# ALiBi and mask tables by 64x64 quadrant matmuls in the first two batches of a fused attention and MLP kernel

## The chip, the cores and the metric

The kernel runs on one core of one Trainium2 chip, and the metric is device time in microseconds (us). A core has a matrix engine (PE, with its weight loads shown apart as PEld), a vector engine (DVE), a scalar engine (ACT), a general engine (POOL), a queue engine (SP) that here only issues transfers, and 16 DMA engines. PE reads operands from the on-chip memory SBUF and writes sums to PSUM, which DVE and ACT read. Each engine works through its own instructions in the order in which they were written; engines wait for one another by semaphores.

## The reference

```python
scores = scale * np.matmul(q, k.transpose(0, 1, 3, 2))        # 8 batches, 8 heads, 576 x 576
rel = pos[:, None] - pos[None, :]
slopes = 2.0 ** (-8.0 * (np.arange(H) + 1) / H)
bias = slopes[:, None, None] * (-np.abs(rel))                 # ALiBi
mask = (rel >= 0) & (rel < 128)                               # causal, sliding window
attn = softmax(np.where(mask, scores + bias, -1e9))
x = (attn @ v)        # to 4608 tokens x 512
h = x @ w_in                                                  # 512 x 2048
out = (h * np.clip(h + 3, 0, 6) / 6) @ w_out                  # 2048 x 512, float32
```

Each query sees itself and the 127 keys before it. So a tile of 128 keys is seen by two tiles of queries: its own ("diagonal", lower triangle) and the next one ("off", the other triangle).

## The kernel before, in words

**Order.** The whole program is written out by hand (`manual_schedule` over all engines): the order of the calls is the order on every engine. `first_batch()` does the attention of batch 0, `second_batch()` that of batch 1 with the first MLP matmuls between, and `segment()` the other six batches, one pair of heads (`g`) at a time, with MLP steps put between by `fill(n)`. An "up" step (`moe_up`, line 532) is four matmuls of 128x512, an ACT relu (line 556) and a DVE product (line 557); a "down" step (`moe_down`, line 587) is four matmuls more. All MLP work of the kernel goes through `fill`.

**Attention of a pair of heads in batches 0 and 1.** Two PSUM tiles of 128 x 2 x 512 (`score`) are used in turn by `score_banks()`. One takes the four diagonal blocks of both heads (`scores_diag`, line 346: eight matmuls, 64 contraction rows, 128 keys, 128 queries), the other the off blocks and the last 64 keys (`scores_off`, lines 372 and 378: ten matmuls). ALiBi and mask come in two ways:

- as a table: `tab` holds slope x (key position - query base), with -2^30 where the mask is; a matmul of the identity with it (lines 321, 357, 360) puts it under the scores in PSUM. So the off blocks of batches 0 and 1 and the diagonal blocks of batch 0;
- as a bias: the diagonal blocks of batch 1 take a per-key bias in the exponential (`exp_diag`, line 425, one of 512 columns per head), and POOL then sets the masked triangle to zero (`affine_select`, line 427). The batches after 1 do this for both kinds of block.

The tables are made at the start by POOL (`base`) and DVE (line 144, eight operations of 128x256), the biases by DVE (lines 166 to 172, seventeen operations of one column). The exponentials go to memory that has no other use yet: `w_out_sb` for batch 0, `gbuf[1]` for batch 1. `attend(g)` then multiplies them with V, DVE divides by the row sum, and `back(g)` turns the result into `xT` for the MLP.

**Batches 2 to 7** already use another score layout in `scores()` (line 399): 64 contraction rows x 64 keys x 192 queries, so that four matmuls have four different quadrants of the PE array. Their rows show what quadrant matmuls do here.

**Around the change.** The first 512 columns of `w_in` come as one transfer issued by SP (`load_raw`) and are cast by POOL and ACT (`cast_raw`, line 187). Loads of `w_out` (`load_w_out`, line 190, four parts of 512 KB) are issued by POOL in `second_batch`, behind whatever POOL has to do before; part p is first read by down step p of the first token block.

Of the kernel before, what the change touches and what calls it, by code (L numbers as in the profile page):

```python
# [13 lines left out]
ALU = mybir.AluOpType  # L14
# [4 lines left out]
def kernel(  # L19
# [39 lines left out]
    tab = perm.tile([128, H, 2, 128], BF16)  # L59
# [63 lines left out]

    def constants():
# [4 lines left out]
        nc.gpsimd.iota(rel_i, pattern=[[0, 1]], base=0, channel_multiplier=1)  # L129
        base = rpool.tile([128, NT], FP32, tag="r6", name="base")  # L130
        base_i = base[:, 0:256].bitcast(INT32).rearrange("p (s c) -> p s c", s=2)
        base_b = base[:, 256:384].bitcast(BF16).rearrange("p (s c) -> p s c", s=2)
        nc.gpsimd.iota(base_i, pattern=[[128, 2], [0, 128]], base=-192, channel_multiplier=1)
        nc.gpsimd.tensor_copy(out=base_b, in_=base_i)
        biases()
        nc.gpsimd.affine_select(out=base_b[:, 1, :], in_=base_b[:, 1, :], pattern=[[1, 128]],
                                channel_multiplier=-1, base=0,
                                compare_op=ALU.is_ge, fill=-(2.0 ** 30))
        nc.gpsimd.affine_select(out=base_b[:, 0, :], in_=base_b[:, 0, :], pattern=[[-1, 128]],
                                channel_multiplier=1, base=-1,  # L140
                                compare_op=ALU.is_ge, fill=-(2.0 ** 30))
        nc.vector.memset(kTb[0][:, :, 4, LAST:128], 0.0)
        for h in range(H):
            nc.vector.tensor_scalar(out=tab[:, h, :, :], in0=base_b, scalar1=slopes[h] / scale,
                                    scalar2=0.0, op0=ALU.mult, op1=ALU.add)
# [5 lines left out]
    def memsets_later():  # L151
        for i in range(2):
            nc.gpsimd.memset(p4buf[i], 1.0)
        nc.gpsimd.memset(kTb[1][:, :, 4, LAST:128], 0.0)
# [10 lines left out]
    def biases():  # L165
        nc.vector.tensor_copy(out=rel_f, in_=rel_i)
        for h in range(H):
            nc.vector.tensor_scalar(out=bias_o[:, h:h + 1], in0=rel_f, scalar1=-192.0,
                                    scalar2=slopes[h], op0=ALU.add, op1=ALU.mult)

        for h in range(H):
            nc.vector.tensor_scalar(out=bias_d[:, h:h + 1], in0=rel_f, scalar1=-64.0,
                                    scalar2=slopes[h], op0=ALU.add, op1=ALU.mult)
# [139 lines left out]
    def diag_tabled(g):  # L313
        return g < NP

    def tables_diag(g):
        scd = score_banks()
        st[g, "scd"] = scd
        for e in range(2 if diag_tabled(g) else 0):
            t = tab[:, 2 * (g % NP) + e, 1:2, :]  # L320
            nc.tensor.matmul(scd[:, e, :].rearrange("p (j c) -> p j c", j=4), lhsT=ident,
                             rhs=t.to_broadcast([128, 4, 128]), start=True, stop=False)

    def rooms(g):
        b, hp = divmod(g, NP)
        if full(g):
            room = w_out_sb if b == 0 else gbuf[1]
            for i, nm in enumerate(("pd", "po")):
                st[g, nm] = room[:, ds(4 * hp + 2 * i, 2), :].rearrange(
                    "p e (j c) -> p e j c", j=4)  # L330
        else:
            st[g, "pd"] = ppool.tile([128, 2, 4, 128], BF16, tag="pd", name="pd")
            st[g, "po"] = ppool.tile([128, 2, 4, 128], BF16, tag="po", name="po")

    def scores_diag(g):
        rooms(g)
        b, hp = divmod(g, NP)
        qT, kT = qTb[b % 2][:, hp, :, :], kTb[b % 2][:, hp, :, :]
        first = not diag_tabled(g)
        if (g, "scd") not in st:  # L340
            tables_diag(g)
        scd = st[g, "scd"]
        for j in range(4):
            for e in range(2):
                r = slice(e * D, (e + 1) * D)
                nc.tensor.matmul(scd[:, e, ts(j, 128)], lhsT=kT[r, j, :],  # L346
                                 rhs=qT[r, j, :], start=first, stop=first or j == 3)

    def tables_off(g):
        hp = g % NP  # L350
        sco = score_banks()
        st[g, "sco"] = sco
        if full(g):
            for e in range(2):
                h = 2 * hp + e
                t = tab[:, h, 0:1, :]
                nc.tensor.matmul(sco[:, e, 128:512].rearrange("p (j c) -> p j c", j=3),  # L357
                                 lhsT=ident, rhs=t.to_broadcast([128, 3, 128]),
                                 start=True, stop=False)
                nc.tensor.matmul(sco[:, e, 0:128].rearrange("p (s c) -> p s c", s=2),  # L360
                                 lhsT=ident, rhs=tab[:, h, :, 0:64], start=False, stop=False)

    def scores_off(g):
        b, hp = divmod(g, NP)
        qT, kT = qTb[b % 2][:, hp, :, :], kTb[b % 2][:, hp, :, :]
# [521 lines left out]
```

## Time and profile before

| | |
|---|---|
| median of three runs | 320.45 us (319.79, 320.45, 320.58) |
| span of the profiled execution | 317.9 us |
| what the runs' median has around that span | 2.55 us |
| PE busy | 307.0 us, 97% |
| ACT, DVE, POOL busy | 196.8, 176.1, 138.9 us |
| granted PE clock | 1.000 |
| first batch, second batch, rest | about 0 to 24.3, 24.3 to 49.7, 49.7 to 317.9 us |

The profiled execution is shown by its span; no time beside the span is given for it. A timeline row gives start and length of a group of instructions, line, operation, output <- inputs, and in brackets how long the engine sat idle before and what ended that. The length of a PE row goes to the modelled end of its last matmul, so the rate is read from one start to the next.

### The profile page before, as it was taken

To read this page: it belongs to the slowest core of one execution; us is meant where nothing else is said; L and a number is where in the kernel's file an instruction comes from. 1 tells how busy PE (TensorE), PEld (TensorE's weight loads), DVE (VectorE), ACT (ScalarE), POOL (GpSimd) and SP (SyncE) were. 2 spreads that over 40 slices of the span, in tenths; PEclk is the share of its full clock that TensorE was granted. 3 is DMA by queue.
4 is the path that set the end of the run, shared out by engine and by line. 5 is a ranking of instruction groups with operands and counts; after the bars stand their busy time and mean duration, and the time that the engine had idled before them with its cause. 6 is when DMAs were issued, how large, how long until landed. Compare 5 with 4: busy or idle time off the path is not lost.

```text
span 317.9 us, 6980 instructions
## 1 busy us (share of the span) xinstructions
PE 307.0 (97%) x2671; PEld 163.4 (51%) x2710; DVE 176.1 (55%) x344; ACT 196.8 (62%) x338; POOL 138.9 (44%) x247
## 2 busy tenths in 40 slices
PE   8889999999999999999999999999999999999996
PEld 3565474455554445555676644454444444444443
DVE  6677676554456654566465546564656455455510
ACT  3869986877767666766667756675764244244401
POOL 7358192674594684548463854472231000000000
PEclk9999999999999999999999999999999999999999
DMA  7999999999999999999999999934112100000112
GB/s 271 264 373 215 255 236 200 236 235 198 216 265 180 222 215 212 213 196 253 186 178 219 190 206 198 228 95 57 49 29 75 66 34 33 35 33 33 66 57 77
DMA packets 131425, 52.43 MB, mean 165 GB/s; under 512 B 118976, under 2 KB 122816, under 8 KB 131392
## 3 DMA queue, kind: packets, MB, share of 16 engines
q1 hardware_dynamic: 125648, 46.15, 69.0%
q0 software_dynamic: 3696, 3.67, 7.1%
q10 hardware_dynamic: 2048, 2.16, 2.2%
q8 instruction: 21, 0.34, 0.5%
q14 instruction: 12, 0.10, 0.1%
HBM read 36.70 MB, written 9.44 MB: 145 GB/s over the span
## 4 chain that ended last, share of the span: by engine, by line
PE 90%; ACT 3%; DVE 3%; issue 2%; POOL 0%; DVEq 0%; POOLq 0%; ACTq 0%
PE hps L532 38%; PE ops L587 37%; PE score L399 3%; PE av L463 2%; PE av L455 2%; DVE avs L485 1%; PE ops L568 1%; PE w L163 1%; ACT w_out_sb L422 1%; PE score L346 1%; PE tp L269 1%; ACT r L556 1%; DVE gbuf L557 1%; PE score L301 1%; PE score L357 1%
## 5 line engine op out<-in xcount | busy, mean ns | idle before, releaser
L556 ACT ACTIVATE r<-hps,bias 128x512 f32<-128x512 f32 x144 | 98.9, 689 | 84.2 <-PE hps L532 83.9
L557 DVE SCALAR_TENSOR_TENSOR gbuf<-r,hps 128x512 bf16<-128x512 f32 x144 | 98.8, 688 | 91.6 <-ACT r L556 90.1
L532 PE MATMUL hps<-xT,w_in_sb 128*128 128x512 bf16 (+1 forms) x623 | 142.0, 358 | 1.7 <-ACT xT L519 0.3
L587 PE MATMUL ops<-w_out_sb,gbuf 128*128 128x512 bf16 x538 | 133.8, 379 | 2.3 <-issue 1.8
L532 PEld LDWEIGHTS <-w_in_sb 128*128 128x128 bf16 x640 | 59.2, 98 | 54.0 <-issue 1.5
L587 PEld LDWEIGHTS <-gbuf 128*128 128x128 bf16 x560 | 52.4, 98 | 57.5
L427 POOL TENSOR_SCALAR_AFFINE_SELECT pd<-pd 128x512 bf16<-128x512 bf16 x48 | 29.4, 631 | 35.2 <-ACT pd L425 35.2
L436 POOL TENSOR_SCALAR_AFFINE_SELECT po<-po 128x512 bf16<-128x512 bf16 x48 | 30.1, 633 | 30.8 <-ACT po L434 30.1
L596 DVE COPY osb<-ops 128x512 f32<-128x512 f32 x33 | 22.7, 688 | 23.8 <-PE ops L587 23.7
L425 ACT ACTIVATE pd<-score,bias_d 128x512 bf16<-128x512 f32 x48 | 31.1, 683 | 6.4 <-PE score L399 6.4
L434 ACT ACTIVATE po<-score,bias_o 128x512 bf16<-128x512 f32 x48 | 33.1, 690 | 0.0
L213 POOL CAST tbuf<-ldbuf 128x512 bf16<-128x512 f32 (+1 forms) x45 | 25.7, 611 | 15.7 <-issue 14.6
L474 DVE TENSOR_TENSOR avs<-av,rc 128x384 bf16<-128x384 f32 (+1 forms) x48 | 23.6, 491 | 1.6
L463 PEld LDWEIGHTS <-pd 128*128 128x128 bf16 x192 | 14.3, 97 | 8.2 <-issue 0.2
L455 PE MATMUL av<-vbuf,po 128*128 128x65 bf16 x192 | 18.0, 193 | 0.0
L206 POOL CAST vbuf<-ldbuf 128x1024 bf16<-128x1024 f32 x14 | 14.3, 1041 | 7.6 <-DMA ldbuf<-in_v_dram 7.6
L463 PE MATMUL av<-vbuf,pd 128*128 128x65 bf16 x192 | 17.3, 194 | 0.0
L455 PEld LDWEIGHTS <-po 128*128 128x128 bf16 x192 | 14.3, 98 | 3.0 <-DVE avs L474 0.5
L439 ACT ACTIVATE p4buf<-score,bias_d 128x64 bf16<-128x64 f32 x48 | 15.6, 324 | 0.0
L399 PEld LDWEIGHTS <-kTb 64*64 64x64 bf16 x480 | 9.4, 106 | 9.1 <-issue 8.5
L399 PE MATMUL score<-qTb,kTb 64*64 64x192 bf16 (+1 forms) x480 | 13.1, 234 | 0.0
L246 POOL CAST pr<-ldbuf 128x576 bf16<-128x576 f32 x18 | 11.5, 668 | 2.6 <-PE tp L238 1.3
(107 smaller groups left out, 201.7 us busy)
## 6 DMA issues: line engine op xcount, KB each, us to landing
out_dram<-osb SPq DMA_DIRECT2D x33, 256.0 KB, 3.5
ldbuf<-in_v_dram SPq DMA_DIRECT2D x31, 256.0 KB, 4.6
ldbuf<-in_q_dram SPq DMA_DIRECT2D x20, 256.0 KB, 5.0
ldbuf<-in_k_dram SPq DMA_DIRECT2D x16, 256.0 KB, 5.3
ldbuf<-in_q_dram SPq DMA_DIRECT2D x12, 288.0 KB, 6.6
ldbuf<-in_k_dram SPq DMA_DIRECT2D x12, 288.0 KB, 6.7
w_out_sb<-in_moe_w_out_dram POOLq DMA_DIRECT2D x4, 512.0 KB, 9.1
w_in_sb<-in_moe_w_in_dram POOLq DMA_DIRECT2D x3, 512.0 KB, 8.8
```

The lines of the kernel that those rows point to most:

```text
L213: nc.gpsimd.tensor_copy(out=tbuf[:m, :, j, :], in_=s[:m, j, :, :].rearrange("p (i e) d -> p i (e d)", e=2))
L399: nc.tensor.matmul(wide[e][c, ds(at, n)], lhsT=kT[r, j, c], rhs=qT[r, ds(q0, n)], start=True, stop=True)
L425: nc.scalar.activation(out=pd[:, e, :, :], in_=block_scores(g, e, False), func=ACT.Exp, bias=bias_d[:, h:h + 1], scale=scale)
L427: nc.gpsimd.affine_select(out=pd[:, e, :, :], in_=pd[:, e, :, :], pattern=[[0, 4], [1, 128]], channel_multiplier=-1, base=0, compare_op=AL ...
L434: nc.scalar.activation(out=po[:, e, :, :], in_=sc, func=ACT.Exp, bias=bias_o[:, h:h + 1], scale=scale)
L436: nc.gpsimd.affine_select(out=po[:, e, :, :], in_=po[:, e, :, :], pattern=[[0, 4], [-1, 128]], channel_multiplier=1, base=-1, compare_op=A ...
L455: nc.tensor.matmul(out_av, lhsT=po[:, e, (qt if full(g) else qt - 1) % 4, :], rhs=vb[:, qt - 1, h, :], start=True, stop=False)
L463: nc.tensor.matmul(out_av, lhsT=d, rhs=vb[:, qt, h, :], start=(qt == 0), stop=True)
L532: nc.tensor.matmul(hps[:, lo:hi], lhsT=w_in_sb[:, ks, ts(ms, 128)], rhs=xT[:, ks, ds(src, hi - lo)], start=(ks == 0), stop=(ks == n_ks - 1))
L556: nc.scalar.activation(out=r6, in_=hps, func=ACT.Relu, bias=bias3[:, 0:1], scale=1.0 / 6.0)
L557: nc.vector.scalar_tensor_tensor(out=gts[nt][:, ms, :], in0=r6, scalar=1.0, in1=hps, op0=ALU.min, op1=ALU.mult)
L587: nc.tensor.matmul(ops[nt, sub], lhsT=gts[nt][:, ms, ts(sub, 128)], rhs=w_out_sb[:, ms, :], start=(ms == 0), stop=(ms == n_ms - 1))
```

## The change

- `tab` becomes 128 x 4 x 3 x 256: for each pair, head e on partitions 64e to 64e+63, three shifts of a strip of 256 (diagonal and off triangle). POOL makes the strip from a cast of six columns with two `affine_select`s of 128x384; DVE scales it by one per-partition slope, four operations of 128x768, one before the first tables, the other three inside `first_batch`.
- Diagonal and off blocks no longer have a PSUM tile each. Half t=0 of a pair holds key tiles 0 and 1 with their diagonal and off blocks side by side, half t=1 key tiles 2, 3 and 4. `tables(g, t)` writes the table by matmuls of 64 contraction rows and 64 output partitions, one quadrant each: four of 512 columns for t=0; for t=1 twelve, in the order quadrant by quadrant, 256, 192 and 64 columns in each. `scores_full` then adds eight (t=0) or ten (t=1) quadrant matmuls of up to 192 columns.
- `exp_full(g, t)`: one exponential of 1024 columns per half, in both batches. Batch 1 loses its eight exponentials of 512 columns with bias and its eight POOL masks, and gains tables under what were its diagonal blocks.
- `biases()` moves from DVE at the start to POOL in `second_batch`, after the cast of V and ahead of `load_w_out(0)`. The zeroing of `kTb[0]` moves from DVE to POOL's `memsets_later`.
- `weights()` finds the block of the exponentials in the new layout; the matmuls with V stay the same in number and size.

```diff
     def constants():
...
-        biases()
...
+        for hp in range(NP):
+            for e in range(2):
+                nc.vector.memset(slope2[ds(e * 64, 64), hp:hp + 1], slopes[2 * hp + e] / scale)
+        nc.vector.tensor_copy(out=first, in_=first_i)
+        wide = first.rearrange("p i s -> p i s ()").to_broadcast([128, 3, 2, 128])
+        nc.gpsimd.affine_select(out=base[:, :, 0, :], in_=wide[:, :, 0, :],
+                                pattern=[[-64, 3], [1, 128]], channel_multiplier=-1, base=64,
                                 compare_op=ALU.is_ge, fill=-(2.0 ** 30))
...
-        nc.vector.memset(kTb[0][:, :, 4, LAST:128], 0.0)
-        for h in range(H):
-            nc.vector.tensor_scalar(out=tab[:, h, :, :], in0=base_b, scalar1=slopes[h] / scale,
-                                    scalar2=0.0, op0=ALU.mult, op1=ALU.add)
+        slope_table(0)
+
+    def slope_table(hp):
+        nc.vector.tensor_scalar(out=tab[:, hp, :, :],
+                                in0=base.rearrange("p i s c -> p i (s c)"),
+                                scalar1=slope2[:, hp:hp + 1],
+                                scalar2=0.0, op0=ALU.mult, op1=ALU.add)
...
+    def tables(g, t):
+        hp = g % NP
+        sc = st[g, "sc", t] = score_banks()
+        for c in range(2):
+            o = slice(c * 64, (c + 1) * 64)
             for e in range(2):
                 r = slice(e * D, (e + 1) * D)
+                src = tab[r, hp, c + 1 - e, :]
+                row = sc[o, e, :]
+                if t == 0:
+                    nc.tensor.matmul(row.rearrange("p (j c) -> p j c", j=2), lhsT=ident[r, r],
+                                     rhs=src.rearrange("p (j c) -> p j c", j=1).to_broadcast(
+                                         [64, 2, 256]), start=True, stop=False)
+                    continue
+                for at, n in ((0, 256), (256, 192), (448, 64)):
+                    nc.tensor.matmul(row[:, ds(at, n)], lhsT=ident[r, r], rhs=src[:, 0:n],
+                                     start=(at == 0), stop=False)
+
+    def scores_full(g, t):
...
+        for j in (2 * t, 2 * t + 1):
+            for c in range(2):
+                q0 = j * 128 + c * 64
+                n = min(192, S - q0)
+                for e in range(2):
+                    r = slice(e * D, (e + 1) * D)
+                    nc.tensor.matmul(sc[ds(c * 64, 64), e, ds(j % 2 * 256 + c * 64, n)],
+                                     lhsT=kT[r, j, ds(c * 64, 64)], rhs=qT[r, ds(q0, n)],
+                                     start=False, stop=(j % 2 == 1 and (t == 0 or c == 1)))
+        if t == 1:
+            for e in range(2):
+                r = slice(e * D, (e + 1) * D)
+                nc.tensor.matmul(sc[0:64, e, 448:512], lhsT=kT[r, 4, 0:64],
+                                 rhs=qT[r, 512:S], start=False, stop=True)
+
+    def exp_full(g, t):
+        at = 1024 * (1 - t)
+        nc.scalar.activation(out=room(g)[:, ds(at, 1024)], in_=st[g, "sc", t].rearrange(
+            "p e c -> p (e c)"), func=ACT.Exp, scale=scale)
...
     def first_batch():
         prepare(0, (V, A))
+        slope_table(1)
...
         prepare(1, (P, V))
+        slope_table(2)
+        slope_table(3)
         transposes(1, (V, V))
...
     def second_batch():
-        scores_diag(NP + 0)
-        exp_diag(NP + 0, 0)
-        exp_diag(NP + 0, 1)
+        scores_full(NP + 0, 0)
+        exp_full(NP + 0, 0)
...
         cast_tokens(1, "v")
-        scores_diag(NP + 2)
-        exp_diag(NP + 2, 0)
-        exp_diag(NP + 2, 1)
+        biases(nc.gpsimd)
+        scores_full(NP + 2, 0)
+        exp_full(NP + 2, 0)
...
         load_w_out(0)
         load_w_out(1)
         g = 2 * NP - 1
-        scores(g)
-        exp_diag(g, 0)
-        exp_diag(g, 1)
-        exp_off_full(g)
+        for t in range(2):
+            scores_full(g, t)
+            exp_full(g, t)
```

More of the change, by code (lines that the diff above doesn't have):

```diff
@@ L153, in memsets_later @@
             nc.gpsimd.memset(p4buf[i], 1.0)
-        nc.gpsimd.memset(kTb[1][:, :, 4, LAST:128], 0.0)
+            nc.gpsimd.memset(kTb[i][:, :, 4, LAST:128], 0.0)
         nc.gpsimd.memset(vbuf[1][:, :, :, D:W], 1.0)
@@ L163, in warm_up, with biases @@
             nc.tensor.matmul(w, lhsT=ident, rhs=rhs, start=True, stop=True)
[L165 to L173, printed above, removed]
+    def biases(eng):
+        eng.tensor_copy(out=rel_f, in_=rel_i)
+        for dst, far in ((bias_o, -192.0), (bias_d, -64.0)):
+            for h in range(H):
+                eng.tensor_scalar(out=dst[:, h:h + 1], in0=rel_f, scalar1=far,
+                                  scalar2=slopes[h], op0=ALU.add, op1=ALU.mult)
     def load_w_in(g):
@@ L311, in full @@
         return g < NB_FULL * NP
[L313 to L324, printed above, removed]
-        b, hp = divmod(g, NP)
[L326 to L343, printed above, removed]
+    def room(g):
+        b, hp = divmod(g, NP)
+        return (w_out_sb if b == 0 else gbuf[1])[:, ds(4 * hp, 4), :].rearrange(
+            "p m c -> p (m c)")
+    def tables(g, t):
[3 more added lines that the diff above has]
+            o = slice(c * 64, (c + 1) * 64)
@@ L344, in scores_diag @@
             for e in range(2):
                 r = slice(e * D, (e + 1) * D)
[L346 to L361, printed above, removed]
```

132 lines of the change are left out of this document (55 added, 77 removed).

## The prediction

> **What bounds the kernel now.** I read the page first, then the busy time by stretches, then the timelines of the first 62 us, where the change lies.
>
> ```profile
> span 317.9 us, 6980 instructions
> PE 307.0 (97%) x2671; PEld 163.4 (51%) x2710; DVE 176.1 (55%) x344; ACT 196.8 (62%) x338; POOL 138.9 (44%) x247
> PE 90%; ACT 3%; DVE 3%; issue 2%; POOL 0%; DVEq 0%; POOLq 0%; ACTq 0%
> ```
>
> ```profile
> 24.00:30.00 6.00, 5.72 (x72) 3.38 (x72) 4.53 (x7) 5.87 (x11) 4.74 (x8) 1.00 1.26 220
> 30.00:40.00 10.00, 9.89 (x80) 4.70 (x79) 6.85 (x10) 9.28 (x15) 3.33 (x5) 1.00 1.16 248
> ```
>
> PE is 97% busy and 90% of the chain that ended last. In the second batch (the two rows: length, then busy time of PE) it is idle for 0.28 of 6 and 0.11 of 10 us. From 24.3 us on, whatever PE does more comes out at the end, and time taken from ACT or POOL is worth only what PE waited for them. The sum is made on the span; the median of the runs, 320.45, has 2.55 us around it, which I keep.
>
> The first batch has a wait of its own:
>
> ```profile
> 18.87 1.14 ACT L187 CAST w_in_sb<-gbuf 128x512 bf16<-128x512 f32 x2 [1.41 <-DMA gbuf<-in_moe_w_in_dram]
> 18.90 0.61 POOL L187 CAST w_in_sb<-gbuf 128x512 bf16<-128x512 f32 x1 [4.66 <-DMA gbuf<-in_moe_w_in_dram]
> 20.60 0.59 PE L532 MATMUL hps<-xT,w_in_sb 128*128 128x512 bf16 x2
> 22.86 0.66 PE L301 MATMUL score<-ident,pr 128*128 128x128 bf16 x9 [0.18 <-ACT pr L256]
> ```
>
> ACT and POOL stand idle until the raw w_in lands at 18.87. Then come two ACT casts, the copies of xT, the cast of q and, at 22.86, the PE work that waits for it. This is why I take the first batch at nothing in both directions: what it gains before 18.87 ends at that transfer, which SP issues untouched; a loss has the 1.41 us of ACT and 0.18 us of PE idle ahead of it.
>
> **The change part by part.** *Start and first batch.*
>
> ```profile
> 2.86 1.76 DVE L144 TENSOR_SCALAR tab<-base 128x256 bf16<-128x256 bf16 x8
> 8.41 0.76 DVE L239 COPY qTb<-tp 128x576 bf16<-128x576 bf16 x1 [0.93 <-PE tp L238]
> ```
>
> Eight table operations of 256 columns took 1.76 us, 0.86 ns a column; a new one of 768 is at most 0.66 us. One replaces eight ahead of the first tables. Two stand ahead of the copy at 8.41, where DVE is idle 0.93 us: 1.32 us would make it 0.4 us late, and the chain copy, scores, exponential with it; the 1.41 us above take that up. The removed DVE biases, the two longer POOL selects and the added POOL memset lie in the same cover. Without it they would cost those 0.4 us. POOL's new wait for the six-column cast holds back only its memsets and the cast of q after them.
>
> *Batch 1 on PE, per pair.* Old blocks:
>
> ```profile
> 34.37 0.40 PE L346 MATMUL score<-qTb,kTb 64*128 64x128 bf16 x8
> 34.70 1.04 PE L532 MATMUL hps<-xT,w_in_sb 128*128 128x512 bf16 x4
> 35.57 0.33 PE L357 MATMUL score<-tab,ident 128*128 128x384 bf16 x1
> ...
> 35.95 0.22 PE L360 MATMUL score<-tab,ident 128*128 128x128 bf16 x1
> 36.11 0.20 PE L372 MATMUL score<-qTb,kTb 64*128 64x64 bf16 x2
> ...
> 36.44 1.90 PE L532 MATMUL hps<-xT,w_in_sb 128*128 128x512 bf16 x8
> ```
>
> Four MLP matmuls go from 34.70 to 35.57, 0.217 us for 512 columns. From 35.95 a table of 128 columns needs 0.054, yet the scores start at 36.11: 0.10 us are lost where the shape changes from 128 to 64 rows, and about as much on the way back. Old cost: diagonal 0.33 + 0.10 = 0.43, off 36.44 - 35.57 = 0.87 us.
>
> What quadrants do, from the scores of batch 2 (the last three rows are what overlaps 49.88 to 49.93, 49.93 to 49.95 and 49.99 to 50.00):
>
> ```profile
> 49.66 0.55 PE L399 MATMUL score<-qTb,kTb 64*64 64x192 bf16 x20
> 50.14 1.04 PE L587 MATMUL ops<-w_out_sb,gbuf 128*128 128x512 bf16 x4
> L399 PE MATMUL score<-qTb,kTb x12: 242/243/268, 49.7 to 49.9; 64*64 64x192 bf16 x12
> L399 PE MATMUL score<-qTb,kTb x15: 216/243/268, 49.7 to 49.9; 64*64 64x192 bf16 x13, 64*64 64x128 bf16 x2
> L399 PE MATMUL score<-qTb,kTb x14: 189/242/243, 49.8 to 50.0; 64*64 64x192 bf16 x10, 64*64 64x128 bf16 x2, 64*64 64x64 bf16 x2
> ```
>
> Twenty matmuls with 3,328 columns take 0.48 us to the next shape, 0.38 without the gap: 1.41 us in a row at the rate above, so four quadrants do work side by side. With three rounds of four begun by 49.93, a round of 192 columns takes 0.08 to 0.09 us.
>
> Half t=0: gap 0.10, four tables side by side 0.22, two rounds 0.17, start 0.02, gap 0.10: 0.60, that is +0.17.
>
> Half t=1 depends on whether the second and third table of a quadrant hold up the next quadrant. The last row: two matmuls of 64 columns had begun by 50.00. They follow, in the code, two of 192 (key half 0) and two of 128 (half 1) that began after 49.93 and so run to about 50.01 and 49.99. As 64-column matmuls of half 0 they would find their quadrant occupied; I read them as those of half 1, which passed two waiting ones. One waiting matmul per quadrant thus doesn't stop the others; the trace doesn't show two. Bounds: all four quadrants free, 245 + 190 ns and the gaps, 0.64 us (-0.23); strictly in order, each quadrant holds the next for 256 + 192 columns, 0.82 of tables, 1.18 us (+0.31). I take the nearest to what is shown: the third weight load of a quadrant waits for its second matmul, so the next quadrant starts 0.13 us behind; the last begins at 0.40, ends tables at 0.64 and scores, partly alongside, at 0.78: 0.98 us (+0.11).
>
> The Trainium skill's page TensorE: Matmul & The Clock Gate, section The mechanism, states that matmuls start and end in program order, "strict FIFO, no reordering". By that rule t=1 would cost the +0.31; the last row above speaks against it.
>
> *ACT and POOL in batch 1.*
>
> ```profile
> 25.36 1.27 ACT L425 ACTIVATE gbuf<-score,bias_d 128x512 bf16<-128x512 f32 x2
> 26.50 1.04 ACT L409 ACTIVATE gbuf<-score 128x1024 bf16<-128x1024 f32 x1
> 26.68 0.66 PE L301 MATMUL score<-ident,pr 128*128 128x128 bf16 x9 [0.23 <-ACT gbuf L425]
> ```
>
> Two exponentials of 512 take 1.27 us, one of 1024 takes 1.04. The 0.23 saved is on the path only here, where PE waited 0.23; so the first pair's +0.28 falls into that wait and comes to 0. Pairs two and three cost 0.28 each. The fourth has its halves back to back, all in 64x64, and saves two shape changes: 0.28 - 0.20 = +0.08. PE sum: +0.64 us. The eight masks gone from POOL are worth nothing in themselves: no PE row waits for one.
>
> *Biases ahead of the w_out loads on POOL.*
>
> ```profile
> L213 POOL CAST tbuf<-ldbuf 128x512 bf16<-128x512 f32 (+1 forms) x45 | 25.7, 611 | 15.7 <-issue 14.6
> L206 POOL CAST vbuf<-ldbuf 128x1024 bf16<-128x1024 f32 x14 | 14.3, 1041 | 7.6 <-DMA ldbuf<-in_v_dram 7.6
> 1.33 0.13 POOL L129 IOTA rel_i<- 128x1 int32 x1
> 1.41 0.34 POOL L133 IOTA base<- 128x256 int32 x1
> 40.06 1.21 POOL L427 TENSOR_SCALAR_AFFINE_SELECT gbuf<-gbuf 128x512 bf16<-128x512 bf16 x2
> 41.23 1.51 POOL L190 DMA_DIRECT2D w_out_sb<-in_moe_w_out_dram x2
> ```
>
> No row has such an operation on POOL. Casts of 512 and 1024 columns (611, 1041 ns) leave 0.18 us for one column; rows of POOL overlap by about 0.05 (41.23 - 40.06 is 1.17 for a row of 1.21), so 0.13 from start to start. Ends: 0.08 (the one-column iota, 1.33 to 1.41) and 0.18 without overlap. Seventeen: 1.4, 2.3, 3.1 us. They replace 1.17 us of masks, so w_out part 0 is issued 0.2, 1.1 or 1.9 us later; I take 1.1. Behind them parts 2 and 3 and the casts come about when they did, since 1.2 us of masks go there too. SP's loads of V for batch 2, which wait for POOL's memset after that, stay with it.
>
> ```profile
> DMA to landing us min/median/max: 11.6/11.6/11.6
> q0 software_dynamic: 1465, 1.46, 116.0%
> q0 software_dynamic: 296, 0.30, 88.1%
> 58.15 1.03 PE L587 MATMUL ops<-w_out_sb,gbuf 128*128 128x512 bf16 x4
> ```
>
> Part 3, issued at 45.89, landed 11.6 us later, at 57.5; its first reader runs at 58.15. These loads are limited by transfer: 1.46 MB from 44 to 52 us, 0.18 MB a us, and 0.15 from 53 to 55 when V loads share (rows two and three). A start 1.1 us later moves 0.2 MB into the slower part: landing about 58.8 to 58.9. The reader, 0.64 us later by PE, wants it at 58.8. So the wait is 0 to 0.2 us; I add 0.15.
>
> Sum: 0 + 0.64 + 0.15 = +0.8 us on 317.9, or 321.25 for the runs.
>
> **The rivals.** *Strict order of quadrants* ends on the slower side: +0.17 + 0.31 per pair, the first pair less the 0.28 that PE's wait and the faster exponential cover, the fourth less 0.2: 0.2 + 0.48 + 0.48 + 0.28 = +1.45 us, 321.9; w_out is then in time. It decides once a quadrant's wait holds back others; for it: the code's order quadrant by quadrant; against: the 64-column row.
>
> *Free quadrants, cheap biases*: t=1 gains 0.23, a pair 0.06; the first pair 0.24 by ACT, the fourth 0.26: -0.6 us, 319.85. It needs the 0.08 us bias too: at 0.13, w_out would land 1.2 us after a reader at 57.55, and the sum is +0.6 again. The skill's page TensorEngine Tiling (Array Packing), section Key Properties, says that tiles load weights and multiply in parallel, independently; by it, this rival. The trace shows it with one waiting matmul only.
>
> *Dear biases*: at 0.18 us part 0 is issued 1.9 us late; 0.35 MB at 0.15 is 2.3, landing at 59.8 to 60.2, +1.7 to +2.1 us: 322.4. For it: the slack of 0.65 us; against: the iota's 0.08.
>
> **How the numbers follow.** Staggered quadrants or late w_out, +0.5 to +1.1: 0.45 (321.25). Strict order: 0.25. Dear biases: 0.17. Free and cheap: 0.13. What a measurement can tell is about 0.3%, 0.96 us. Faster by more than that takes the last case and more gain than I find, or a first-batch gain that gets past the transfer: 0.09. Slower: rivals one and three, and the upper part of the likeliest: 0.50. Within: 0.41. Range 319.8 to 322.6, from the free case to just past the dear one; the likeliest's own is 320.95 to 321.6.
>
> **What would show it.** Second batch starting near 24.3 again. A t=0 block of 0.60 and a t=1 block of 0.98 us between MLP matmuls (0.64 or 1.18 by the rivals). Seventeen POOL rows taking about 2.3 us from 40.1, and PE's first read of w_out part 3 with or without idle time. I am wrong if the first batch moves the start of the second, if the quadrants behave otherwise in a row of twelve, or if POOL's small operations cost several times an iota.

## The result, and the profile after

The changed kernel takes 322.83 us (median of four runs, 322.50 to 323.05) against 320.14 us for the kernel before (319.79 to 320.58): a ratio of 1.0075, with a 95% interval of 1.0054 to 1.0097. It is slower, the side that had the largest chance (0.50). The predicted time, 321.25, was too low by 1.6 us, and the range ended at 322.6, 0.2 below the measured time. The profiled execution has a span of 321.0 us and took 322.78; the one before had a span of 317.9, 3.1 us less.

The page of the kernel after: the span, the busy time of each engine, and the shares of the chain that ended last.

```profile
span 321.0 us, 7140 instructions
PE 304.6 (95%) x2759; PEld 162.3 (51%) x2798; DVE 175.5 (55%) x331; ACT 196.1 (61%) x334; POOL 137.1 (43%) x256
PE 79%; DMA 11%; POOL 3%; DVE 2%; issue 2%; SPq 1%; ACT 0%; POOLq 0%
```

PE has 88 matmuls more and is busy 2.4 us less, yet the end comes later; transfers and POOL now hold 14% of the chain, where PE alone had 90%. So PE's own work was not what got dearer. Where the 3.1 us come in can be read from the starts of the groups that both kernels have (all in us; "second batch" is its first PE row, the others are the scores of four groups of batches 2 to 4):

| | second batch | batch 2, first | batch 2, second | group near 103 | group near 111 |
|---|---|---|---|---|---|
| before | 24.32 | 49.66 | 59.97 | 103.21 | 111.24 |
| after | 24.77 | 49.51 | 60.71 | 104.75 | 114.38 |
| later by | 0.45 | -0.15 | 0.75 | 1.54 | 3.14 |

From 114 us to the end nothing is added. There are five steps: 0.45 late into the second batch, 0.60 gained in it, then 0.90, 0.80 and 1.60 lost at three places.

**The gain.** The timeline of PE after, one pair of the second batch (start, length, and what runs):

```profile
34.54 0.41 PE L334 MATMUL score<-tab,ident 64*64 64x512 bf16 x4
34.78 0.34 PE L355 MATMUL score<-qTb,kTb 64*64 64x192 bf16 x8
35.05 1.04 PE L505 MATMUL hps<-xT,w_in_sb 128*128 128x512 bf16 x4
36.02 0.42 PE L339 MATMUL score<-tab,ident 64*64 64x256 bf16 x11
36.26 0.25 PE L355 MATMUL score<-qTb,kTb 64*64 64x192 bf16 x1
36.26 0.19 PE L339 MATMUL score<-tab,ident 64*64 64x64 bf16 x1
36.27 0.33 PE L355 MATMUL score<-qTb,kTb 64*64 64x192 bf16 x7
```

The half t=0 goes from 34.54 to 35.05, with the 0.10 us of the shape change ahead of it 0.61. The half t=1 starts at 36.02 and the next MLP matmul at 36.56: with the shape change 0.64 us. All twelve tables have begun by 36.26, and the first score matmul begins with the last table, not behind it. Nor do the tables begin in the order of the code, which writes 256, 192 and 64 columns for one quadrant before it goes to the next. These are the table matmuls that overlap 36.02 to 36.08 and 36.18 to 36.22:

```profile
L339 PE MATMUL score<-tab,ident x4: 293/293/293, 36.0 to 36.0; 64*64 64x256 bf16 x4
L339 PE MATMUL score<-tab,ident x8: 243/268/293, 36.0 to 36.2; 64*64 64x256 bf16 x4, 64*64 64x192 bf16 x4
```

The first piece of all four quadrants has begun before any second piece, and all four second pieces before any third.

**The losses.** First POOL's timeline after, then the rows of before that answer to its last two (the w_out row of before, at 41.23, stands in the prediction).

```profile
39.95 0.18 POOL L175 CAST rel_f<-rel_i 128x1 f32<-128x1 int32 x1
40.23 1.65 POOL L178 TENSOR_SCALAR bias_o<-rel_f 128x1 f32<-128x1 f32 x8
41.83 1.69 POOL L178 TENSOR_SCALAR bias_d<-rel_f 128x1 f32<-128x1 f32 x8
43.46 1.52 POOL L196 DMA_DIRECT2D w_out_sb<-in_moe_w_out_dram  x2
50.09 0.10 POOL L745 MEMSET ldbuf<- 128x1 f32 x1
61.92 1.04 POOL L212 CAST vbuf<-ldbuf 128x1024 bf16<-128x1024 f32 x1 [2.15 <-DMA ldbuf<-in_v_dram]
```

```profile
49.06 0.10 POOL L768 MEMSET ldbuf<- 128x1 f32 x1
59.35 1.04 POOL L206 CAST vbuf<-ldbuf 128x1024 bf16<-128x1024 f32 x1
```

The seventeen biases hold POOL from 39.95 to 43.46: 3.5 us, 0.2 us each. The first w_out load is issued 2.2 us later than before (43.46 against 41.23), the memset for which SP's loads of V for batch 2 wait comes 1.0 us later, and V is cast 2.6 us later. SP's rows of these loads, after and then before:

```profile
50.22 11.42 SPq L118 DMA_DIRECT2D ldbuf<-in_v_dram  x5
```

```profile
49.18 9.58 SPq L117 DMA_DIRECT2D ldbuf<-in_v_dram  x5
```

PE's timeline after shows who pays, in the brackets (idle time before the row, and what ended it):

```profile
52.70 1.02 PE L560 MATMUL ops<-w_out_sb,gbuf 128*128 128x512 bf16 x4 [0.54 <-DMA w_out_sb<-in_moe_w_out_dram]
58.90 1.02 PE L560 MATMUL ops<-w_out_sb,gbuf 128*128 128x512 bf16 x4 [0.40 <-DMA w_out_sb<-in_moe_w_out_dram]
64.78 0.19 PE L436 MATMUL av<-vbuf,pd 128*128 128x65 bf16 x1 [0.98 <-POOL vbuf L212]
107.50 0.20 PE L436 MATMUL av<-vbuf,pd 128*128 128x65 bf16 x1 [0.34 <-POOL pd L397]
108.08 0.20 PE L434 MATMUL av<-vbuf,po 128*128 128x65 bf16 x1 [0.38 <-POOL po L406]
108.67 0.20 PE L434 MATMUL av<-vbuf,po 128*128 128x65 bf16 x1 [0.35 <-POOL po L406]
```

Two reads of w_out wait (the 0.90), one of V (the 0.80), and near 108 us three products wait for POOL's masks (the 1.60; the brackets are smaller, since they count from the modelled end of the matmul before and not from its start). Those masks stand behind a cast that stands behind SP's transpose of q. Rows of SP and POOL, after and then before:

```profile
97.20 4.08 SPq L224 DMA_TRANSPOSE qTb<-tbuf  x1
103.43 2.83 POOL L219 CAST tbuf<-ldbuf 128x512 bf16<-128x512 f32 x5 [5.82 <-issue]
106.22 1.22 POOL L397 TENSOR_SCALAR_AFFINE_SELECT pd<-pd 128x512 bf16<-128x512 bf16 x2
```

```profile
94.86 3.78 SPq L218 DMA_TRANSPOSE qTb<-tbuf  x1
100.09 2.83 POOL L213 CAST tbuf<-ldbuf 128x512 bf16<-128x512 f32 x5 [4.03 <-issue]
102.88 1.21 POOL L427 TENSOR_SCALAR_AFFINE_SELECT pd<-pd 128x512 bf16<-128x512 bf16 x2
```

The transpose reads `tbuf`, which the cast overwrites. It was issued 2.3 us later than before, since SP has been behind from the late V loads on (its next loads of q start at 64.31 instead of 61.43), and it took 6.1 us to land where it had taken 5.1; 103.43 and 100.09 are just behind the two landings. The cast is 3.3 us late and PE, itself 1.5 late by then, loses 1.6 more.

### The profile page after: what moved, and what is told of

It reads as the page before. It is cut to its first block, busy times and chain, and to the rows that moved or that the text cites. A ratio compares the mean times of both kernels' runs of the same rounds, so it can differ in the third digit from the quotient of the medians.

```text
span 321.0 us, 7140 instructions
## 1 busy us (share of the span) xinstructions
PE 304.6 (95%) x2759; PEld 162.3 (51%) x2798; DVE 175.5 (55%) x331; ACT 196.1 (61%) x334; POOL 137.1 (43%) x256
## 4 chain that ended last, share of the span: by engine, by line
PE 79%; DMA 11%; POOL 3%; DVE 2%; issue 2%; SPq 1%; ACT 0%; POOLq 0%
PE ops L560 36%; PE hps L505 33%; PE score L385 3%; DMA ldbuf<-in_q_dram 3%; DMA ldbuf<-in_v_dram 3%; DMA w_out_sb<-in_moe_w_out_dram 3%; DMA ldbuf<-in_k_dram 2%; PE av L436 2%; PE av L434 2%; SPq L106 1%; POOL pr L252 1%; PE ops L541 1%; PE tp L275 1%; POOL tbuf L219 1%; POOL w_in_sb L182 0%
```

## The experiments

The theory after these rows: the quadrants give the gain that they can give, and all of the loss is queued behind POOL's seventeen small operations: w_out, then V, then through SP's queue the transposes. The rivals: the new layout itself costs time; the biases cost wherever they stand; the late masks near 105 us are a thing of their own.

**The biases back on DVE.**

```diff
         nc.vector.tensor_copy(out=first, in_=first_i)
+        biases(nc.vector)
...
         cast_tokens(1, "v")
-        biases(nc.gpsimd)
```

> The changed kernel with one thing undone: the seventeen bias operations are on DVE again, at the start, while DVE waits for POOL's selects. Queue theory (the biases on POOL put off the w_out loads by 2.2 us and the loads of V for batch 2 by 1 us, and all that PE loses after 50 us comes from that; the tables and scores by quadrants gain about 0.6 us in the second batch): PE waits for w_out, V and the late masks near 107 us are gone, and the time is 0.6 us below the kernel before, less up to 0.45 us if the raw w_in again lands late: 0.998 to 1.000 of before. Table theory (the new layout, its tables or the longer exponentials cost it): still slower than before by 1.5 us or more, 1.005 and above.

Measured: 320.26 us (319.86 to 322.45) against 320.28, a ratio of 1.0000 (0.9976 to 1.0024). POOL issues w_out at 40.36. The loss in time is gone, and no gain is left over. One read of w_out still waits 0.4 us, and three products near 106 us lose 1.1, two of them in these rows:

```profile
106.55 0.20 PE L435 MATMUL av<-vbuf,po 128*128 128x65 bf16 x1 [0.38 <-POOL po L407]
107.14 0.20 PE L435 MATMUL av<-vbuf,po 128*128 128x65 bf16 x1 [0.35 <-POOL po L407]
```

So the loss hangs on the biases' place, but the wait for masks does not hang on it alone.

**The kernel before, with the same seventeen operations on POOL at the same place** (into a tile that nobody reads).

```diff
         cast_tokens(1, "v")
+        biases_pool()
         scores_diag(NP + 2)
```

> The kernel before with one thing added: the seventeen bias operations a second time, into memory that nothing reads, on POOL in the place where the changed kernel has them, ahead of the loads of w_out. Queue theory: 3.5 us more on POOL with nothing taken away (the changed kernel put them in the place of 1.2 us of masks), so w_out, the gate of V and the queue behind come 3.5 us late instead of 2.2 and 1.0: PE loses 3 to 6 us, 1.010 to 1.018 of before. Table theory: no difference that can be measured, 0.998 to 1.003, since no table is touched.

Measured: 322.96 us (322.27 to 324.82), a ratio of 1.0079 (1.0050 to 1.0109). They cost the kernel before as much as the whole change costs, though less than the 1.010 to 1.018 that were expected. The first to pay is another, though: here POOL still has batch 1's masks behind them, and PE waits for these.

```profile
40.78 3.27 POOL L182 TENSOR_SCALAR bias_g<-rel_g 128x1 f32<-128x1 f32 x16
45.17 1.52 POOL L200 DMA_DIRECT2D w_out_sb<-in_moe_w_out_dram  x2
44.69 0.20 PE L473 MATMUL score<-vbuf,gbuf 128*128 128x65 bf16 x1 [1.08 <-POOL gbuf L437]
```

So this run shows the price of 3.5 us on POOL at that place, not the same chain of waits.

**The biases on POOL, but behind the gate, and between w_out and the gate.** The gate is POOL's memset of one column of `ldbuf[2]`, for which SP's loads of V of batch 2 wait.

```diff
         load_w_out(2)
         load_w_out(3)
+        biases(nc.gpsimd)                         # second of the two runs
         prepare_double(2, 1, (P, P))
         nc.gpsimd.memset(ldbuf[2][:, 0:1], 0.0)
+        biases(nc.gpsimd)                         # first of the two runs
```

> The changed kernel with the seventeen bias operations still on POOL, but behind the small memset that lets the loads of V for batch 2 go, where POOL stands idle until the first mask of batch 2. Queue theory: as fast as with the biases on DVE, 0.998 to 1.001 of before, since nothing is queued behind them; they have to be done by the first exponential of batch 2 near 53 us. If it is the work on POOL itself (its share of memory ports) and not its place: as slow as the changed kernel, 1.005 to 1.010.

> The changed kernel with the seventeen bias operations on POOL behind the last load of w_out and ahead of the casts and the memset that lets the loads of V for batch 2 go. This parts the two delays. If the late w_out alone makes the loss (with all that comes after): no PE wait for w_out, and 0.998 to 1.001 of before. If the late loads of V make part of it through the SP queue: w_out is in time, but V comes about 2.4 us later than before (3.5 less the 1.2 of the masks taken away), PE waits for its cast near 64 us and for late masks near 107 us as in the changed kernel, 1.003 to 1.009 of before.

Measured: 320.77 us, a ratio of 0.9998 (0.9974 to 1.0021; the two medians themselves, 320.77 and 320.28, are 0.15% apart), and 320.20 us, 0.9995 (0.9966 to 1.0023). The same 3.5 us of POOL cost nothing that can be measured when no w_out load stands behind them. The gate's place shows in SP's queue, in the row of V's five loads, of the first and then of the second of the two:

```profile
46.51 11.93 SPq L118 DMA_DIRECT2D ldbuf<-in_v_dram  x5
```

```profile
49.78 7.84 SPq L118 DMA_DIRECT2D ldbuf<-in_v_dram  x5
```

Issued 3.3 us earlier, V's loads share the transfers with w_out and are through SP later, at 58.4 instead of 57.6. In both runs no read of w_out waits. The second run does not delay V alone, as it was meant to: with w_out issued earlier, at 39.51, the gate comes only 0.6 us later than before, not 2.4.

```profile
49.64 0.12 POOL L745 MEMSET ldbuf<- 128x1 f32 x1
```

That is 0.45 us ahead of the changed kernel's gate (50.09), yet V's five loads take 7.84 us instead of 11.42. So what made V late in the changed kernel was mostly the late w_out that its loads met, and not the late gate. This table counts from the second batch's start, so that the start itself drops out:

| us from the start of the second batch to | batch 2, first | batch 2, second | near 103 | near 111 |
|---|---|---|---|---|
| before | 25.34 | 35.65 | 78.89 | 86.92 |
| after | 24.74 | 35.94 | 79.98 | 89.61 |
| biases on DVE | 25.02 | 35.85 | 79.03 | 88.22 |
| biases behind the gate | 24.86 | 35.09 | 78.34 | 88.23 |
| biases between w_out and gate | 24.61 | 34.85 | 78.02 | 86.98 |

Between w_out and gate the new layout is 0.87 us ahead at 103 us, and has lost it at 111. The stretch between these two groups takes 8.03 us before, 9.63 after, and 9.19, 9.89 and 8.96 in the other three: the wait for masks comes in every one of these profiles of the new layout, wherever the biases are. So at most a part of the 1.60 us can be put down to the biases. What is left to find is this second loss.

**The order of the table matmuls.** On the last of these kernels (the base from here on), the twelve tables of t=1 piece by piece over the quadrants.

```diff
-            for at, n in ((0, 256), (256, 192), (448, 64)):   # inside a quadrant
+        for at, n in ((0, 256), (256, 192), (448, 64)) if t == 1 else ():
+            for c in range(2):
+                for e in range(2):
```

> On top of the same kernel, the twelve table matmuls of the half t=1 are written piece by piece (all four quadrants with 256 columns, then all with 192, then all with 64) instead of quadrant by quadrant. If matmuls of different quadrants don't wait for one another, however many are waiting in one quadrant, the block from the last MLP matmul to the next takes the same 0.64 us. If matmuls start in the order of the code, the old order would have taken 1.18 and the new one would take about 0.64; since the old one took 0.64, this theory is already in trouble, and a new order that is shorter than 0.64 by more than 0.05 would be its last support. If a fixed number can wait (the staggered case of the prediction), the new order would gain up to 0.3 us.

```profile
35.84 0.41 PE L341 MATMUL score<-tab,ident 64*64 64x256 bf16 x12
36.08 0.33 PE L358 MATMUL score<-qTb,kTb 64*64 64x192 bf16 x8
36.38 1.90 PE L508 MATMUL hps<-xT,w_in_sb 128*128 128x512 bf16 x7
```

From 35.84 to 36.38, 0.54 us (36.02 to 36.56 in the other order): the order of the code makes no difference. This run is read by its trace alone; it was executed once. Two matmuls waiting in one quadrant don't hold up the next quadrant; neither a strict nor a staggered order is left.

**The cast of k taken from ahead of the masks.** On the base, the cast of k of batch 4 and its transpose go between the off masks of the two heads.

```diff
-        elif nb < B and nb > 3 and hp < 2:
+        elif nb < B and nb > 3 and hp < 2 and g != 13:
...
                 exp_off(g, 0)
+            if g == 14:
+                cast_tokens(4, "k")
+                xbar(4, "k")
```

> On top of the kernel with the biases between the w_out loads and POOL's gate memset, POOL's cast of k of batch 4 (five pieces, 2.83 us, it waits for the transpose of q to free tbuf) and SP's transpose behind it are moved from ahead of the masks of the group scored at 94 us to between its off masks of head 0 and head 1. Theory (the free quadrants gain 0.5 to 0.7 us, and it is given back near 105 us because the masks queue behind a cast that waits for SP's transposes): PE's two gaps of 0.40 and 0.52 us at 105.2 and 105.8 are gone, the scores that stood at 111.51 come at 110.5 to 110.7 (before: 111.24), and the kernel takes 319.5 to 319.8, a ratio of 0.998 to before. Rival (the wait belongs to the chain exponential, mask, product of that group and not to the cast): the gaps stay at 0.8 to 1.0 us together, 320.2. A third way: the transpose of k, now about 0.3 us later, becomes the wait of the next group's scores: a gap ahead of them at 110.6 instead, no gain.

```profile
105.36 4.57 SPq L224 DMA_TRANSPOSE kTb<-tbuf  x1
111.96 0.55 PE L385 MATMUL score<-qTb,kTb 64*64 64x192 bf16 x20 [0.62 <-DMA kTb<-tbuf]
```

Measured: 319.43 us (319.15 to 322.02) against 320.53, a ratio of 0.9974 (0.9948 to 1.0000). The gaps near 105 us are gone, so the cast was what held the masks. The third way came true with it: the scores wait for k's transpose and come 86.80 us after the second batch's start, where the next run, without this wait, has 86.05. The time is the lowest of a full kernel here, with an interval that ends at no change.

**V's last two loads put behind that transpose.**

> On top of the kernel with the k cast between the masks: SP's last two loads of V of batch 4 go behind the transpose of k instead of ahead of it. That run's new wait, 0.78 us of PE ahead of the scores at 111.96, is put down to the transpose of k starting at 105.36 behind five V loads (100.24, 4.36 us) and one store. Theory: with two loads fewer ahead of it the transpose starts at 104.4 to 104.7, as soon as the cast is done, and the gap ahead of the scores shrinks from 0.78 to 0.1 (the shape change alone) or up to 0.3; from the second batch's first table to the group near 111 us, PE takes 86.1 to 86.3 us (before 86.92 from its first scores, 87.19 with the biases ahead of the w_out loads behind; the last run 86.80), and the kernel 319.0 to 319.5. Rival: the transpose is late for another reason (its own 4.57 us, the store ahead of it): the gap stays above 0.6 and the time at 319.4 to 319.8.

```profile
103.89 3.50 SPq L224 DMA_TRANSPOSE kTb<-tbuf  x1
110.73 0.55 PE L385 MATMUL score<-qTb,kTb 64*64 64x192 bf16 x20
122.65 1.24 PE L505 MATMUL hps<-xT,w_in_sb 128*128 128x512 bf16 x5 [0.55 <-DMA xT<-avs]
```

Measured: 320.07 us, a ratio of 0.9980 (0.9958 to 1.0003); the 319.0 to 319.5 that were expected are not reached. The scores come after 86.05 us without a wait, as the theory had it, and the next one waits: the MLP step at 122.65, for another transpose of SP's queue. Each time the wait has only moved along that queue.

**Less in SP's queue, for both kernels.** The twelve stores of the first three token blocks are left out, in the base and in the kernel before; both leave those rows of the output unwritten.

```diff
                 nc.vector.tensor_copy(out=osb, in_=ops[nt, sub])
-                nc.sync.dma_start(out=out[rows, :], in_=osb)
+                if nt > 2:
+                    nc.sync.dma_start(out=out[rows, :], in_=osb)
```

> The kernel with the biases between the w_out loads and POOL's gate memset, without the stores of the first three token blocks (twelve stores of 256 KB, which SP issues between about 69 and 150 us; those rows of the output are not written). Theory (the gain of the quadrants, 0.87 us from the second batch's first table to the scores near 102.5 us, is given back because the queue of SP and the transfers behind it have no room between 84 and 112 us): without the stores SP's transpose of q starts about 1.5 to 2 us sooner, the cast behind it and the masks too, PE's gaps of 0.40 and 0.52 us near 105.5 are gone, and the 0.87 us still stand at the group near 111 us, counted from the start of the second batch. Against the kernel before without the same stores the time is 0.6 to 0.9 us less, a ratio of 0.997 to 0.998. Rival (the wait comes from the order of POOL's work and the length of the transposes themselves, 4.5 us against 3.8, and not from what is queued ahead): the gaps stay, 0.7 to 1.0 us, and the two kernels without stores are equal within 0.2 us.

> The control: the kernel before without the same twelve stores. Its PE waits for nothing near 105 us and lies 86.92 us from the second batch's first scores to the group at 111.24, so the stores that are gone should change nothing there: 86.8 to 87.0 us for that stretch, and 319.6 to 320.4 for the whole, within 0.3% of before. If it is faster by more than 0.5 us, the kernel before too is held by transfers somewhere else, and the other run has to be read against this one alone.

The first two rows are of the base without the stores, the third of the kernel before without them:

```profile
92.74 3.17 SPq L224 DMA_TRANSPOSE qTb<-tbuf  x1
110.46 0.55 PE L385 MATMUL score<-qTb,kTb 64*64 64x192 bf16 x20
```

```profile
112.34 0.55 PE L399 MATMUL score<-qTb,kTb 64*64 64x192 bf16 x20
```

Measured: 319.22 us, a ratio to the whole kernel before of 0.9975 (0.9963 to 0.9986); the kernel before without the stores takes 320.37, 1.0012 (0.9999 to 1.0026). The new layout without the stores has 86.04 us up to the group near 111, no wait for masks, and of the 0.88 us that it is ahead there keeps 0.7 to the end. q's transpose takes 6.6 us to land here too; it is only issued 1.2 us earlier than in the base. The old layout gains nothing from the same room: 87.19 us (0.27 of it in the second batch, above the 86.8 to 87.0 that were expected; why, these rows don't tell). So the gain of the quadrants is real, and it is taken back in SP's queue and the transfers behind it; the stores fill both, so these runs don't part the two.

**Why q's transpose lands late.** In the base it is issued 0.95 us earlier than in the kernel before and lands 6.5 us after its issue instead of 5.1. One theory was the place of the buffers, which the larger tables move by 2 KB: an unused tile of that size in the kernel before, and one of 2 KB more in the base.

```diff
+    pad = perm.tile([128, 525], FP32)             # before; [128, 512] in the base
     rel_i = perm.tile([128, 1], INT32)
```

> The kernel before with one unused tile of 2,100 bytes per partition behind its tables (one column of it is set to zero at the start), so that every buffer behind lies where it lies in the changed kernel, whose tables are 2 KB larger. What it is for: SP's transpose of q of batch 4 landed 5.1, 5.2 and 5.1 us after its issue in the three profiles with the old tables and 5.8 to 7.1 us in the eight with the new ones; the transpose of k that follows, 6.7 to 7.3 against 4.8 to 5.3 (6.6 in one). Theory (the place of the buffers in memory sets it): q lands after 6.0 to 7.0 us and k after 4.8 to 5.4; the cast behind q's transpose starts near 101 instead of 100.09, and PE gets a gap of 0.3 to 0.9 us near 106 as in the changed kernel, 320.4 to 321. Rival (what else is in flight at that moment sets it): 5.1 and 6.7 to 7.3 us as before, no gap, 320.2.

> The kernel with the biases between the w_out loads and POOL's gate memset, with an unused tile of 2 KB per partition behind its tables, so that the buffers behind lie 2 KB further than in the changed kernel and about 4 KB further than before. Theory (the place of the buffers sets the landing of the transposes): q's landing moves away from 6.5 us, to near 5.1 if only the place within 4 KB counts, and PE's gaps of 0.40 and 0.52 us near 105.5 go with it. Rival: it stays at 6 to 7 us, with the gaps, and the time at 320.2.

Measured: 320.19 us, 1.0008 (0.9987 to 1.0028), q landing after 5.3 us and k after 7.0; and 320.26 us, 1.0002 (0.9978 to 1.0026), q after 7.1 us and k after 4.9. That theory falls. Another came from the view of the transfers: during the late transposes a packet of the queue q8 passes, which brings instructions, and in the kernel before it passes during k's transpose. The count of q8 over the whole run, of before and then of after, speaks for PE's instructions, of which after has more, where DVE and ACT have fewer:

```profile
q8 instruction: 21, 0.34, 0.5%
```

```profile
q8 instruction: 22, 0.36, 0.5%
```

By estimate from these rows, 0.34 MB on 5,381 matmuls and weight loads are 63 bytes each, 0.36 on 5,557 are 65. The last run moves these packets by 42 matmuls more in the warm-up.

```diff
-        warm_up(5)
+        warm_up(3)
+        small_matmuls(14)                         # 32 columns, nobody reads them
...
-        warm_up(3)
+        small_matmuls(33)
```

> The kernel with the biases between the w_out loads and POOL's gate memset, with 42 matmuls more in the warm-up of PE at the start (in place of five of 512 columns, 47 of 32 columns, whose results nobody reads). It moves the transfers of the instruction queue q8, which brings 0.36 MB in 22 packets where the kernel before has 0.34 MB in 21 and PE 88 matmuls fewer: those in the profile of this base come at 84.5, 96.0 and 112.0 us, and 42 matmuls with their weight loads should bring the one of 96.0 forward by 3 to 4.5 us, to where the kernel before has it (92.5). Theory (a transpose during which such a packet is fetched takes longer: in the profiles so far the large transposes without one land after 4.8 to 5.7 us in most cases, those with one after 6 to 7.6): q's transpose of batch 4 lands after 5.0 to 5.7 us instead of 6.5, the cast behind it starts at 99 to 99.6 instead of 100.56, the masks too are 1.0 to 1.4 us earlier, PE's gaps near 105.5 shrink from 0.92 to at most 0.1 us, and the 0.87 us gained in the second batch still stand at the group near 111 us: 319.1 to 319.6, a ratio of 0.997 to 0.998. Rival (the fetch only happens to fall there): the packet moves and the landing stays at 6 to 7 us, with the gaps and 320.2. If the packet doesn't move out of the transpose, the run says nothing on either.

The transpose of q in this run (issue in SP's queue, and its landing by the view of the tile), POOL's cast, and the group:

```profile
93.70 3.61 SPq L229 DMA_TRANSPOSE qTb<-tbuf  x1
DMA to landing us min/median/max: 5.0/5.0/5.0
98.85 2.84 POOL L224 CAST tbuf<-ldbuf 128x512 bf16<-128x512 f32 x5 [3.37 <-issue]
```

The packet that began between 96.0 and 96.5 in the base now begins between 91.5 and 92.0, and the one behind it, between 106.0 and 106.5, falls into k's transpose, which takes 7.0 us to land. q lands after 5.0, the cast starts 1.7 us earlier than in the base, PE waits for no mask, and the scores near 111 come at 110.64, 0.60 us ahead of the kernel before and ahead by that to the end of the trace (span 317.3). The timed runs do not follow: 320.05 us (319.07 to 322.41), a ratio of 1.0007 (0.9986 to 1.0027), where 0.997 to 0.998 was expected. The profiled execution, 319.07, is the fastest of twelve, and five of them take 320.5 to 322.4. So the link from packet to transpose to cast to PE is shown in one pair of traces; that it decides the time of the kernel is not. What made the other executions of this program longer was not profiled.

## Why the prediction was right or wrong

*First batch at nothing.* The second batch starts 0.45 us later than before, since the raw w_in landed at 19.32 instead of 18.87. Over the fourteen profiles of both layouts it starts between 24.14 and 25.16; the old layout alone spans 24.14 to 25.16. So the 0.45 us are not shown to come from the change, and the difference of the two profiles contains them all the same.

*Quadrants.* t=0 was right: 0.60 predicted, 0.61 measured. t=1 was wrong: 0.98 predicted, 0.64 measured. The step that failed is "the third weight load of a quadrant waits for its second matmul, so the next quadrant starts 0.13 us behind". The prediction had read one waiting matmul per quadrant from batch 2's scores and taken the nearest case to that as the likeliest; the free case was the rival, and its working is borne out: -0.6 us predicted for PE, -0.60 measured from the start of the second batch to batch 2 (25.34 to 24.74). The rule "strict FIFO, no reordering" of the Trainium skill (TensorE: Matmul & The Clock Gate, The mechanism) does not hold for this trace: it would give 1.18 us where 0.64 are measured, and the tables began piece by piece over the quadrants although the code writes them quadrant by quadrant. The independent tiles of the Trainium skill's page TensorEngine Tiling (Array Packing), Key Properties, agree with the trace. One count in the prediction's reading of batch 2 is wrong and changes nothing: the twenty score matmuls have 3,200 columns (14 of 192, 2 of 128, 4 of 64), not 3,328.

*Biases.* The mechanism was right, the size was not: 0.13 us each was predicted with 0.18 as the upper end, 0.2 measured; the seventeen take 3.5 us, not 2.3. The lower end came from an iota, which is another operation; the upper, from casts of 512 and 1024 columns drawn out to one column, was still too low, so it was no bound. w_out was issued 2.2 us later instead of 1.1, and its readers lose 0.90 us instead of 0.15: two of them wait, where only the last was looked at.

*"SP's loads of V for batch 2, which wait for POOL's memset after that, stay with it."* This cost that was set at nothing is the first that the sum lacks. The memset was 1.0 us late and V's loads took 11.4 us instead of 9.6; PE lost 0.80 us. The run with the biases between w_out and the gate puts most of that on the late w_out.

*What nothing in the sum spoke of:* the masks near 108 us, 1.60 us and the largest term. "From 24.3 us on, whatever PE does more comes out at the end" was read as if PE alone bounded the rest. The row of the transfers on the page of before says otherwise, in tenths of 40 slices:

```profile
DMA  7999999999999999999999999934112100000112
```

The transfers were at 90% or more up to 200 us. SP's queue had as little room as PE, and a later landing of q's transpose met POOL's order of casts and masks some 60 us behind the edit. How much of the 1.60 us the biases added stays open: with the biases elsewhere, the new layout lost 0.93 to 1.86 us in the same stretch.

*The sum.* 0.45 - 0.60 + 0.90 + 0.80 + 1.60 = 3.15 for the two profiles, against 0.8 predicted. The sign and most of the time were those of the rival of dear biases (322.4, chance 0.17), by its cause; its PE term was too high by 1.2 us, and it lacked V and the masks. That the forecast lay on the slower side was in part luck: 0.64 of its 0.8 us were PE's, and there the change gained. The range ended just past that rival, and so just short. The terms add up to the 3.1 us between the two profiles, while the medians are 2.7 us apart. Executions whose span is on record took 1.66 to 1.79 us more than that span, so a span of 317.9 belongs to an execution about half a microsecond faster than the median of the kernel before.

## What to carry to other kernels

Small operations put on an engine that also issues loads are priced by what is queued behind them: here 3.5 us on POOL cost 0.75 to 0.8% ahead of the w_out loads and nothing that could be measured behind them. Before a gain on the busiest engine is counted to the end, look at the row of the transfers and at the queue that issues them; where they are full too, the gain needs room there, as the runs without stores showed. An upper bound for the cost of an operation that the trace lacks should not be extrapolated from large ones of another kind.

## What the runs showed of the hardware that was not expected

- Matmuls in different 64x64 quadrants did not wait for one another, even with two more waiting in each quadrant: twelve tables and ten score matmuls took 0.54 us between two shape changes, in either order of the code, and they began in another order than that of the code.
- One-column operations on POOL took 0.2 us from start to start (sixteen from 40.23 to 43.46 us), about a third of a cast of 512 columns (0.61).
- A transpose of 20 blocks by SP's queue landed after 4.8 to 5.7 us in most cases without an instruction packet in flight, and mostly after 6 to 7.6 us with one; exceptions stand on both sides (eight with one at 4.9 to 5.8, two without at 6.2 and 6.6). In about half of the long ones (28 of 53) the packet begins only 4.4 to 5.2 us after the issue, when a short transpose has landed or is about to, so this count alone doesn't tell which holds up the other. Moving the packet out of one transpose brought that from 6.5 to 5.0 us and lengthened the next to 7.0. With the 88 matmuls added to PE these packets fall elsewhere: in the batch looked at here, two came in the half microseconds from 92.5 and 108.0 in the kernel before, and from 96.0 and 112.0 in the base.
